# A linear-attention and mixture-of-experts kernel on one core: its computed instruction order replaced by a written-out table

## The chip, the cores and the metric

One Trainium2 chip, one of its cores. The metric is device time in microseconds (us) of one execution; the runs shown give a median and their lowest and highest.

## The reference

Inputs are q, k, v of shape (4, 8, 768, 64) (batch, heads, sequence, head size) and the weights of a four-expert layer. First comes retention, a linear attention with a decaying state; its output, 512 wide, is the x of the second part. There every expert is a causal softmax attention over x with a head of 64; a gate picks two experts for each token and mixes their outputs.

```python
for t in range(S):
    state = gamma[None, :, None, None] * state + np.einsum('bhd,bhe->bhde', k[:, :, t], v[:, :, t])
    y[:, :, t] = scale * np.einsum('bhd,bhde->bhe', q[:, :, t], state)
x = y.transpose(0, 2, 1, 3).reshape(B, S, H * D)
logits = x @ w_gate
# top 2 of 4 experts per token, softmax over the two: w
for e in range(E):
    q, k, v = x @ wq[e], x @ wk[e], x @ wv[e]
    scores = scale * (q @ k.transpose(0, 2, 1))      # causal mask, softmax over keys: a
    out += (weight of e for each token) * (a @ v @ wo[e])
```

## The kernel before, in words

**Retention** runs in 24 chunks of 128 tokens, six to a batch. `chunk` makes three operations on PE (TensorE) of it: `h1`, `h2`, `h1`. `h1` adds 64 tokens to the state in `ps_st` (L486, a matmul of k and v from the tile `kv_t`) and multiplies q with the state so far (L490); the two kinds alternate, 16 calls. In a batch's last `h1` only L490 is left, in its first only L486, 8 calls each. `h2` alternates the products inside a chunk (L545) with the score blocks of the next chunk (L551), 32 calls. All of them are matmuls of 64x64 tiles of float32; one call makes two matmul instructions and two weight loads. So a whole chunk is 64 calls, and where a batch ends and the next begins the two last pieces and the first ones can stand one behind the other. Before a chunk can start, SP must load its `kv_t` (`load`, L414, 512 KB) and `qkT_t` (L410), and POOL (GpSimd) must scale k (`kdecay`, L425) and q (`qdecay`, L440). After each `h1` DVE (VectorE) copies the state out, scaled (L500); after `h2` it masks the score blocks (L559).

**Projections.** Half a batch (384 tokens) is one stage j, eight in all. Its x, split into a rounded part `xh` (ACT, ScalarE, L513) and a rest `xl` (DVE, L516), is multiplied with the weights: `proj` (L601, 12 matmuls for a pair p of experts and e in the pair) gives q and k, `vgate` (L643, 12 matmuls) gives v and the gate's logits. ACT and DVE bring q and k to SBUF (L606, L609), and SP shifts halves of them between partitions by DMA (`move`, L618): two `q<-k`, one `k<-q` that overwrites what the `q<-k` have read and so waits for their landing, one `k<-k`.

**Softmax.** `mpass` (L738, L724, L737) computes scores for the row maximum alone, which DVE takes (L746, L727); `mrow` transposes the maxima on PE (L774), ACT copies them (L776), and SP sends them through DRAM (L778, L780) into row 64 of the q tiles. `score` computes the scores again with that row as an extra term (L850, L851), ACT takes the exponential (L857), `av` multiplies with v (L896). `norm_a` sums over keys on PE (L919, 24 calls of 32 columns), the factors go through DRAM (L933, L937), `norm_b` applies them (POOL, ACT), `wout` (L1010) is the last product, and SP stores 128 rows of the output (L1020).

PE changes its tiling between these: 64x64 for the chunks, 128x64 for L896, 128x32 for L919, 128x128 for the rest. PSUM has six banks for everything passing (`ps`) and one each for the state (`ps_st`) and for L896 (`ps_o`).

**What sets the order.** No operation is emitted at once. `op` records each of them (1,555) with engine, cost, what it reads and writes, and which buffers it begins. `schedule` then plays the program with those costs: at each step, of the operations ready on an engine, the one with the lowest start plus a hundredth of its rank is taken; `shift` has moved the ranks by random numbers of 66 seeds. The result is one list, and it fixes for each engine, SP's queue included, the order in which its instructions stand; each engine works strictly through its own. It also fixes which of a tag's buffers an operation gets. All DMAs are issued by SP, which issues one only when its data and buffer are ready and when the eighth DMA before it has landed; what is queued behind it waits with it.

```python
sc = max(s, T[e]) + ALPHA * o.rank
if e == "PE" and o.mode != mode:
    sc += SWP * SWITCH
...
order = R.schedule()
with tc.manual_schedule():
    for o in order:
        o.fn()
```

## Time and profile before

| | |
|---|---|
| median of 3 runs | 330.72 us (329.74 to 331.65) |
| span of the profiled execution, first to last instruction | 326.7 us |
| median less span (what lies around the instructions) | 4.0 us |
| PE busy with matmuls | 314.3 us, 96% |
| PE weight loads | 272.9 us, 84% |
| DVE, ACT, POOL busy | 53%, 41%, 52% |
| share of PE on the chain that ended last | 88% |
| granted PE clock | full speed, 0.999 in the mean |
| DMA | 50.8 MB, 156 GB/s in the mean |

The profile gives the profiled execution by its span. Busy time of PE counts matmuls that overlap, so a busy engine can still issue more slowly than it might; the distance between two starts tells that. Idle time of an engine that is not the bottleneck costs nothing. "Issue" in the chain is time in which an engine waited for nothing that the profile shows.

### The profile page before, as it was taken

To read this page: it belongs to the slowest core of one execution; us is meant where nothing else is said; L and a number is where in the kernel's file an instruction comes from. 1 tells how busy PE (TensorE), PEld (TensorE's weight loads), DVE (VectorE), ACT (ScalarE), POOL (GpSimd) and SP (SyncE) were. 2 spreads that over 40 slices of the span, in tenths; PEclk is the share of its full clock that TensorE was granted. 3 is DMA by queue.
4 is the path that set the end of the run, shared out by engine and by line. 5 is a ranking of instruction groups with operands and counts; after the bars stand their busy time and mean duration, and the time that the engine had idled before them with its cause. 6 is when DMAs were issued, how large, how long until landed. Compare 5 with 4: busy or idle time off the path is not lost.

```text
span 326.7 us, 11233 instructions
## 1 busy us (share of the span) xinstructions
PE 314.3 (96%) x4738; PEld 272.9 (84%) x4738; DVE 174.7 (53%) x478; ACT 132.6 (41%) x322; POOL 170.3 (52%) x189
## 2 busy tenths in 40 slices
PE   7779999999999999999999999999999999999995
PEld 3669989889978799879979788897979789878674
DVE  2574467666443555767242574937452243896733
ACT  1452222533535333524527224432534235428542
POOL 5776251561874976314785854542394361913700
PEclk9999999999999999999999999999999999999999
DMA  7996993355468353535563675352412422413022
GB/s 261 357 403 226 283 324 117 112 142 179 106 188 266 136 181 102 161 124 181 145 160 135 197 237 144 142 164 86 114 45 99 98 49 74 125 69 91 1 99 96
DMA packets 22071, 50.82 MB, mean 156 GB/s; under 512 B 3618, under 2 KB 8310, under 8 KB 22020
## 3 DMA queue, kind: packets, MB, share of 16 engines
q1 hardware_dynamic: 22020, 50.10, 49.0%
q8 instruction: 37, 0.61, 0.8%
q14 instruction: 14, 0.11, 0.1%
HBM read 30.71 MB, written 6.79 MB: 115 GB/s over the span
## 4 chain that ended last, share of the span: by engine, by line
PE 88%; DMA 7%; issue 1%; SPq 1%; DVE 1%; ACT 1%; ACTq 0%
PE ps L601 20%; PE ps L1010 11%; PE ps_o L896 11%; PE ps L643 9%; PE ps L850 7%; PE ps L851 6%; PE ps_st L486 5%; PE ps L551 4%; PE ps L738 4%; DMA kv_t<-in_kv_dram 3%; PE ps L545 2%; DMA qkT_t<-in_qkT_dram 2%; PE ps L490 2%; PE ps L919 2%; PE ps L724 2%; PE ps_st L896 1%
## 5 line engine op out<-in xcount | busy, mean ns | idle before, releaser
L746 DVE CUSTOM_DVE_ANT_0 scr<-ps,cmask_t 128x128 bf16<-128x128 f32 (+3 forms) x64 | 29.7, 487 | 46.6 <-PE ps L738 46.1
L857 ACT ACTIVATE pt<-ps 128x384 f32<-128x384 f32 (+2 forms) x112 | 49.4, 491 | 12.1 <-PE ps L851 9.7
L440 POOL TENSOR_TENSOR qd<-qkT_t,qdec_t 128x512 f32<-128x512 f32 (+1 forms) x23 | 28.3, 1232 | 41.4 <-PE ps L490 26.2
L601 PE MATMUL ps<-xh,qk_hi 128*128 128x384 f32 x128 | 44.1, 345 | 0.0
L850 PE MATMUL ps<-q,k 128*128 128x384 f32 (+2 forms) x144 | 43.4, 316 | 0.0
L601 PE MATMUL ps<-xh,qk_lo 128*128 128x384 f32 x128 | 43.1, 337 | 0.0
L601 PE MATMUL ps<-xl,qk_hi 128*128 128x384 f32 x128 | 43.1, 336 | 0.0
L851 PE MATMUL ps<-q,k 65*128 65x384 f32 (+2 forms) x144 | 42.1, 312 | 0.0
L879 POOL TENSOR_TENSOR ac<-ac,pt 128x256 f32<-128x256 f32 (+2 forms) x32 | 39.9, 1247 | 3.1 <-ACT pt L857 1.2
L863 POOL TENSOR_SCALAR_AFFINE_SELECT pt<-pt 128x256 f32<-128x256 f32 x48 | 20.1, 426 | 38.9 <-ACT pt L857 38.2
L896 PE MATMUL ps_o<-pt,vt 128*64 128x384 f32 (+2 forms) x252 | 36.2, 422 | 0.0
L606 ACT ACTIVATE k<-ps 128x384 fp32r<-128x384 f32 x32 | 15.7, 491 | 50.0 <-PE ps L601 50.0
L425 POOL TENSOR_TENSOR kv_t<-kv_t,kdec_t 128x512 f32<-128x512 f32 (+1 forms) x23 | 22.2, 968 | 23.0 <-DMA kv_t<-in_kv_dram 23.0
L486 PE MATMUL ps_st<-kv_t 64*64 64x64 f32 x704 | 30.2, 222 | 1.7 <-POOL kv_t L425 0.7
L490 PE MATMUL ps<-qd,sblk 64*64 64x64 f32 x704 | 29.8, 221 | 0.8 <-issue 0.8
L872 POOL TENSOR_TENSOR ac<-pt,pt 128x512 f32<-128x512 f32 (+1 forms) x14 | 21.3, 1523 | 17.5 <-ACT pt L857 17.1
L486 PEld LDWEIGHTS ps_st<-kv_t 64*64 64x64 f32 x704 | 24.9, 134 | 6.2 <-issue 4.0
L896 PEld LDWEIGHTS ps_o<-pt,vt 128*64 128x64 f32 x252 | 16.4, 136 | 16.0 <-issue 11.9
L513 ACT ACTIVATE xh<-ps 128x512 fp32r<-128x512 f32 x24 | 14.3, 598 | 37.4 <-PE ps L490 35.6
L643 PE MATMUL ps<-vg_hi,xh 128*128 128x260 f32 x96 | 28.0, 291 | 1.5 <-ACT xh L513 1.5
L850 PEld LDWEIGHTS ps<-q,k 128*128 128x128 f32 x144 | 27.3, 190 | 2.4 <-issue 2.0
L500 DVE TENSOR_TENSOR sblk<-ps_st,sdec_t 128x256 f32<-128x256 f32 x44 | 18.5, 420 | 19.8 <-PE ps_st L486 18.4
(115 smaller groups left out, 777.6 us busy)
## 6 DMA issues: line engine op xcount, KB each, us to landing
qkT_t<-in_qkT_dram SPq DMA_DIRECT2D x24, 512.0 KB
kv_t<-in_kv_dram SPq DMA_DIRECT2D x24, 512.0 KB
out_dram<-ot SPq DMA_DIRECT2D x24, 256.0 KB
q<-k SPq DMA_DIRECT2D x28, 192.0 KB
k<-k SPq DMA_DIRECT2D x14, 192.0 KB
k<-q SPq DMA_DIRECT2D x14, 192.0 KB
fe<-fd SPq DMA_DIRECT2D x28, 96.0 KB
pt<-in_wqk_dram SPq DMA_DIRECT2D x4, 256.0 KB
```

Of the source, the lines that this page charges most:

```text
L440: e.tensor_tensor(halves(qd.t), halves(qb.t[:, 0]), K["qdec"][:, :, None, :].to_broadcast([128, HP, n, SC]), op=OP.mult)
L486: nc.tensor.matmul(ST[b].t[rows(rt), s * D:(s + 1) * D], kvs(m, 0, s)[rows(rt)], kvs(m, 1, s)[rows(rt)], start=c == 0 and s == 0, stop=Fal ...
L490: nc.tensor.matmul(yo(m, rt, s), SB[m % 2][rows(rt), s], LD[g, 2].t[rows(rt), s, m % 2 * SC:(m % 2 + 1) * SC], start=m % 2 == 0 and s == 0 ...
L601: nc.tensor.matmul(pb.t[:, :HS], ww[:, kt, wsl], xx[:, kt], start=n == 0, stop=n == 11)
L643: nc.tensor.matmul(pb.t[:, :NV + E], xx[:, kt, sl], ww[:, kt], start=n == 0, stop=n == 11)
L746: lambda: nc.vector.tensor_tensor_reduce(scr.t[:, :n1], pb.t[:, :n1], K["cmask"][:, HS + C - n1:], 1.0, mx0.t[:, e, i:i + 1] if prior else ...
L850: nc.tensor.matmul(o, k1.t[:, e, ko:ko + C], q1.t[:, e, q0:], start=True, stop=False)
L851: nc.tensor.matmul(o, k2.t[:65, e, ko:ko + C], q2.t[:65, e, q0:], start=False, stop=True)
L857: lambda es=es, sb=sb, n=n: nc.scalar.activation(pt.t[:, es[0]:es[0] + n, q0:], sb.t[:, :n * w].rearrange("p (e t) -> p e t", e=n), AF.Exp ...
L879: op(eng, cost, lambda: en.tensor_tensor(ac.t[:, :, q0:], ac.t[:, :, q0:], pt.t[:, :, q0:], op=OP.add), r=[(pt, 0), (pt, 1), (ac, "b")], w ...
L896: nc.tensor.matmul(ob.t[e * 64:e * 64 + 64, q0:HS], vt.t[:, ko // C, ee * 64:ee * 64 + 64], pt.t[:, e, q0:], start=kb == 0, stop=kb == las ...
L1010: nc.tensor.matmul(wb.t, oo[:, sl], ww[:, p], start=n == 0 and p == 0, stop=n == 2 and p == NP - 1)
```

## The change

`shift`, `by_path`, `schedule` and `replay` go, with their constants. In their place stands a table of 1,555 numbers, `ORDER`, and for each tag a string of digits, `SLOTS`, that says which buffer each operation's new tile gets; `arrange` lists the operations by them. What is computed, the number of instructions and their shapes stay. For each engine, the operations up to the table's 108th stand as they did; from there on they are moved against each other, on PE by 2.2 places in the mean and 22 at most (510 operations). PE keeps its order for its first 27 operations, up to 39.0 us of the profile before; SP for its first 31, up to 29.9 us.

```diff
@@ -119,155 +95,14 @@
-    def by_path(self, first, scale):
...
-    def shift(self, seeds):
...
-    def schedule(self):
...
+    def arrange(self, order, slots):
+
+        turns = {name: iter(row) for name, row in slots.items()}
+        out = [self.ops[i] for i in order]
+        for o in out:
             for b in o.new:
...
+                b.slot = int(next(turns[b.tag.name]))
         return out
@@ -1160,19 +995,136 @@
-    if PATH:
-        R.by_path(first, PATH)
-    R.shift(SHIFTS)
-    order = R.schedule()
     with tc.manual_schedule():
-        for o in order:
+        for o in R.arrange(ORDER, SLOTS):
             o.fn()
 
+
+ORDER = (
+    2, 1, 3, 4, 5, 6, 7, 8, 9, 10, 11, 12, 13, 14, 15, 16, 17, 18, 81, 22, 19, 20, 0, 21, 23, 99, 100, 101, 102, 103,
...
+SLOTS = {
+    "ac": "010101010101010101",
...
```

The lines of the functions move up by 165 with it: L486 of before is L321 now, L618 is L453.

**First place, PE where the first batch ends and the second begins.** Before (L490 the last piece of the old batch, L486 the first of the new, L551 and L545 the `h2` that follows):

```order
L545 MATMUL ps_142<-am_72,kv_t_68 64x64
L490 MATMUL ps_142<-qd_70,sblk_156 64x64 x8
L486 MATMUL ps_st_147<-kv_t_66 64x64 x8
L551 MATMUL ps_143<-qkT_t_64 64x64
L545 MATMUL ps_140<-am_71,kv_t_66 64x64
```

Now (L325 and L321 are the same two pieces, L573 is `mpass`, L478 is `vgate`):

```order
L380 MATMUL ps_143<-am_72,kv_t_68 64x64
L325 MATMUL ps_143<-qd_70,sblk_156 64x64 x8
L321 MATMUL ps_st_147<-kv_t_66 64x64 x8
L573 MATMUL ps_145<-k_0_83,q_0_77 128x256
L573 MATMUL ps_144<-k_0_83,q_0_77 128x256
L478 MATMUL ps_142<-vg_hi,xh_74 128x260
L478 MATMUL ps_142<-vg_lo,xh_74 128x260
L478 MATMUL ps_142<-vg_hi,xl_76 128x260
```

Before, `h2` and the second `h1` of the new batch's first chunk follow at once, 48 calls; now two `mpass`, a `vgate`, two more `mpass`, a `proj` and a transpose stand ahead of them. At the two other borders of batches `h2` and `h1` followed at once too; now matmuls of L896 (and at the third border an L919 behind them) come between. PE has 76 runs of one tiling before and 82 now.

**Second place, SP's queue around the load of chunk 6, the second batch's first** (`kv_t_66`; L618, now L453, is `move`). Before:

```order
L618 DMA q_0_77<-k_0_83 64x768
L618 DMA k_0_88<-k_0_83 64x768
L618 DMA q_0_77<-k_0_83 64x768
L410 DMA qkT_t_64<-in_qkT_dram 128x1024
L414 DMA kv_t_66<-in_kv_dram 128x1024
L618 DMA k_0_83<-q_0_80 64x768
L618 DMA q_1_78<-k_1_84 64x768 x2
L618 DMA k_1_89<-k_1_84 64x768
```

Now:

```order
L453 DMA q_0_77<-k_0_83 64x768 x2
L245 DMA qkT_t_64<-in_qkT_dram 128x1024
L453 DMA k_0_83<-q_0_80 64x768
L249 DMA kv_t_66<-in_kv_dram 128x1024
L453 DMA k_0_88<-k_0_83 64x768
L453 DMA q_1_78<-k_1_84 64x768 x2
L245 DMA qkT_t_65<-in_qkT_dram 128x1024
L453 DMA k_1_89<-k_1_84 64x768
```

The load of `kv_t_66` stood ahead of the `k<-q` move (`k_0_83<-q_0_80`) and stands behind it now; one `k<-k` move went from ahead of both to behind them. A little further on, the two small transfers of the first mask of maxima (L778, L780), which stood behind two loads and three moves, stand ahead of the next `kv_t` load now, and the first `score` (L850, L851), which reads what they bring, has moved up on PE: between its transpose (L774) and it stand `h2` and `h1` of chunk 6, four `mpass` and a `proj`.

**Third place, SP's queue at the moves of a later stage** (`q_1_78<-k_2_85` and `k_2_85<-q_1_81` are its `q<-k` and `k<-q`; `fe` are the loads of the softmax factors, L937, now L772). Before:

```order
L618 DMA k_2_90<-k_2_85 64x768
L618 DMA q_1_78<-k_2_85 64x768
L937 DMA fe_126<-fd_139 64x384
L618 DMA q_1_78<-k_2_85 64x768
L937 DMA fe_126<-fd_139 64x384 x2
L618 DMA k_2_85<-q_1_81 64x768
L937 DMA fe_126<-fd_139 64x384
L778 DMA md_137<-mt_107 6x128
L780 DMA q_0_80<-md_137 1x768
```

Now:

```order
L453 DMA q_1_78<-k_2_85 64x768 x2
L453 DMA k_2_85<-q_1_81 64x768
L772 DMA fe_126<-fd_139 64x384 x4
L613 DMA md_137<-mt_107 6x128
L453 DMA q_2_79<-k_0_83 64x768
L615 DMA q_0_80<-md_137 1x768
L453 DMA q_2_79<-k_0_83 64x768
L855 DMA out_dram<-ot_128 128x512
```

The two `q<-k` and the `k<-q` stood between the four `fe` loads and stand ahead of all of them now. On PE, the first `mpass` that needs the `k<-q` has the 12 matmuls of another `proj` (L601, now L436) ahead of it that came after it before. The last L919 that followed a chunk's 64 calls at once, at 224.7 us, has four other operations between now; one of an earlier stage, at 73 us, has come to stand behind a chunk.

## Rows read from the trace of the kernel before

**Rows 1.** The page: PE's busy line, and the queue that brings instructions.

```profile
PE 314.3 (96%) x4738; PEld 272.9 (84%) x4738; DVE 174.7 (53%) x478; ACT 132.6 (41%) x322; POOL 170.3 (52%) x189
...
q8 instruction: 37, 0.61, 0.8%
```

**Rows 2.** Busy time by stretch: length, then each engine's, clock, DMA share, GB/s.

```profile
40.00:280.00 240.00, 237.63 (x3676) 212.08 (x3676) 126.04 (x354) 97.25 (x239) 130.67 (x139) 1.00 0.48 146
```

**Rows 3.** The same view, of four stretches of 64x64 matmuls.

```profile
43.09:45.94 2.85, 2.10 (x103) 1.75 (x99) 1.93 (x4) 0.51 (x1) 2.17 (x2) 1.00 0.91 255
94.27:96.29 2.02, 2.02 (x129) 1.95 (x128) 1.44 (x6) 0.47 (x1) 0.74 (x2) 1.00 0.71 256
110.61:112.36 1.75, 1.75 (x102) 1.62 (x98) 1.52 (x4) 0.51 (x1) 1.67 (x2) 1.00 0.69 176
186.41:188.95 2.54, 2.07 (x103) 1.81 (x99) 1.86 (x4) 0.51 (x1) 1.88 (x2) 1.00 0.82 235
```

**Rows 4.** Timeline of PE at borders: start us, us, engine line op.

```profile
39.04 0.34 PE L643 MATMUL ps<-vg_hi,xh 128*128 128x260 f32 x1
...
40.54 0.40 PE L738 MATMUL ps<-k,q 128*128 128x256 f32 x2
40.87 0.27 PE L486 MATMUL ps_st<-kv_t 64*64 64x64 f32 x1
...
50.90 0.41 PE L738 MATMUL ps<-k,q 128*128 128x256 f32 x2
51.15 0.29 PE L643 MATMUL ps<-vg_hi,xh 128*128 128x260 f32 x1
...
94.78 0.22 PE L551 MATMUL ps<-qkT_t 64*64 64x64 f32 x1
...
261.06 0.27 PE L774 MATMUL ps<-ident_t,mx 128*128 128x128 f32 x1
```

**Rows 5.** The chain that ended last: start us, us, what.

```profile
44.75 0.75 issue
...
147.11 0.79 PE ps L919 x24
...
188.10 0.47 issue
...
192.21 2.10 PE ps L601 x12
...
224.70 0.78 PE ps L919 x21
225.48 0.38 issue
225.86 0.41 PE ps L919 x3
```

**Rows 6.** PE's waits: engine line waited for, us in total, times, longest.

```profile
PE ps L738 <- DMA k<-q: 0.8, 1, 0.8
```

**Rows 7.** Timeline of SP: DMA issues at two places.

```profile
30.58 0.59 SPq L618 DMA_DIRECT2D q<-k  x1
...
31.91 0.52 SPq L414 DMA_DIRECT2D kv_t<-in_kv_dram  x1
35.17 0.47 SPq L618 DMA_DIRECT2D k<-q  x1
...
261.66 0.29 SPq L778 DMA_DIRECT2D md<-mt  x1
262.86 0.25 SPq L780 DMA_DIRECT2D q<-md  x1
```

**Rows 8.** Timeline of POOL around 38 us; in brackets idle before, releaser.

```profile
37.59 0.74 POOL L440 TENSOR_TENSOR qd<-qkT_t,qdec_t 128x256 f32<-128x256 f32 x1 [4.70 <-DMA kv_t<-in_kv_dram]
38.28 1.04 POOL L425 TENSOR_TENSOR kv_t<-kv_t,kdec_t 128x512 f32<-128x512 f32 x1
```

**Rows 9.** SP's own waits, as in rows 6.

```profile
SPq L780 <- DMA md<-mt: 12.1, 9, 2.1
```

## The prediction

> **What bounds the kernel now.** I read the page of the profile first. PE is busy for 96% of the span [rows 1], so only three things can move the time: idle time of PE, time in which it issues more slowly than it could, and what the first 39 us and the last few hold, which the change hardly touches (PE's order is the same up to 39.0 us). Then the busy time by stretch: between 40 and 280 us PE is idle for 240 - 237.63 = 2.4 us [rows 2]. That is all that better-placed waits can win there, so I looked inside the busy time as well, at starts on the timeline and at the chain of waits.

> The 64x64 matmuls show what is to be found. An ordinary chunk, 64 calls, takes 2.02 us [rows 3]. Its `h2` begins at 94.78 [rows 4], so `h2` and the last `h1`, 48 calls, take 96.29 - 94.78 = 1.51 us. Where one batch ends and the next begins, the same 48 calls follow 64 others at once, and there they take 2.85, 1.75 and 2.54 us [rows 3]. In two of the three PE stands still for 0.75 and 0.47 us with "issue" as the reason [rows 5], waiting for nothing that the profile shows; the rest of the excess is slower issue. A third stop of this kind, 0.38 us, cuts an L919 in two; that one also follows a chunk's 64 calls at once [rows 5].

> What could be late there is the program itself. The queue that brings instructions moved 0.61 MB in 37 transfers [rows 1]; over PE's 4738 matmuls and as many weight loads that is 64 bytes each, so an estimated 256 instructions to a transfer. An ordinary chunk uses up 257 (129 and 128) in 2.02 us [rows 3]; the whole program takes one transfer in 326.7 / 37 = 8.8 us. So a chunk eats instructions four times as fast as the mean, and only a second dense piece right behind it has shown a stop.

> **The change, part by part.**

> *Dense runs are taken apart.* At all three borders `h2` and `h1` now stand behind other work. Before, they took 2.85 + 1.75 + 2.54 = 7.14 us; standing alone I take the ordinary 1.51 each, 4.53. That wins 2.6 us. It costs six more changes of PE's tiling (76 runs become 82). Two L738 of 256 columns take 51.15 - 50.90 = 0.25 us when the same tiling follows and 40.87 - 40.54 = 0.33 when a 64x64 run does [rows 4], 0.08 more, which I round up to 0.1 a change and 0.6 in all. Net -2.0. The other end: if the stops stay wherever the matmuls stand, only the slower issue goes, and the net is near 0.

> [...]

> *L919 away from a chunk.* The 24 calls of an L919 take 0.79 us when nothing stops them, and 0.78 + 0.38 + 0.41 = 1.57 at 224.7 [rows 5]. With four operations between, I take the 0.78 as won. The other end is 0: an L919 at 73 us has come to stand behind a chunk, and it may stop there. I take the gain since the one at 147.11, also right behind a chunk, was not stopped [rows 5].

> *The wait for a `k<-q`.* One L738 waits 0.8 us for that DMA [rows 6]. Now the moves go ahead of the factor loads in SP's queue, and a `proj` of 2.10 us [rows 5] stands ahead of the L738. That covers the 0.8 whole: -0.8, with 0 as the other end if the moves are later than before. The factor loads that are passed have slack: they feed POOL, and PE reads of them much later.

> *A load behind a move.* The load of `kv_t` for chunk 6 was issued at 31.91 and ended POOL's wait just before 37.59, 5.7 us later [rows 7, 8]. Now it stands behind the `k<-q`, which was issued at 35.17 [rows 7] since it waits for the `q<-k` of 30.58 to land; that one moves up by one issue, 0.6 us. So the load goes at 35.1 to 35.7 and lands, after the same 5.7 us, at 40.8 to 41.4; L425 on POOL adds 1.04 [rows 8]. PE meanwhile has brought the old batch's last chunk forward: it started at 40.87, behind the `vgate` of 39.04 [rows 4], and starts at 39.1 now; the new batch's first L486 came an estimated 1.8 us after that start (2.22 to the `h2` at 43.09 [rows 3], less 0.4 for itself), so PE stands before it at 40.9. It waits for 0.9 to 1.5 us if the flight is as long as it was. Between that and 0, if the load flies faster with less ahead of it, I take 0.8. Behind this L486 all of PE waits.

> *The first row of maxima.* The first `score` has moved up. From L774 to L778 takes 0.6 us, and the next transfer L780 goes 1.2 us later [rows 4, 7]; with as much again for its landing the way takes 3.0. SP's waits for such a transfer reach 2.1 us, 2.4 with its issue [rows 9], which makes 0.6 + 2.4 + 2.4 = 5.4. Between the transpose and the first use PE now has 1.51 for `h2` and `h1`, 2.10 for a `proj`, 0.2 for two changes of tiling and an estimated 0.6 for four `mpass` and the first L850: 4.4 us. So the wait is 0 to 1.0. DMA is 0.91 busy around there [rows 3], which speaks for the slow end: +0.4.

> *Swaps on DVE and ACT.* Neighbours changed places all over both queues; their work is the same. In a queue that waits in order, a swap makes PE wait for at most the instruction that was let ahead, about 0.48 us on DVE (1.93 for four) or 0.51 on ACT [rows 3]. I found three places where PE reads right behind such a swap: a `proj` behind `xl` near 44 us, a `vgate` that needs a PSUM bank back near 61, an L896 near 305. A third of 0.5 each makes +0.5, with 0 and 1.5 as ends.

> *Removed code* runs on no engine: the planner worked while the kernel was built. Cost 0.

> **The sum:** -2.0 - 0.8 - 0.8 + 0.8 + 0.4 + 0.5 = -1.9 us. The profiled span of 326.7 becomes 324.8. The runs' median, 330.72, is 4.0 above the span, and I leave those 4.0 as they are: **328.8 us**, 0.6% less. About 0.5%, 1.65 us, is what a measurement of this kernel can tell from no change.

> **Rivals.**

> *The stops move instead of going.* If the "issue" stops come from where transfers of instructions begin and end and not from how dense the calls stand, other places will be hit. For it: the middle border had no stop with the same 112 calls [rows 3], and the third border's `h2` now stands right behind an L919, 72 calls in a row. Against it: in 40 to 280 us every stop was behind more than 64 dense calls. Then 0.75 + 0.47 + 0.78 = 2.0 us of the gain are gone: 330.8, no change. [...] Rows 5 show the stops, no row their cause.

> *Lateness is handed on in SP's queue (slower).* All loads go through one queue, and a `k<-q` that waits holds everything behind it. If the `kv_t` load is not only late once, but the next two, which use the two other buffers of that tile, are late behind it, PE pays at three chunks. It decides at 39.9 us: a load that lands later than that (40.9 less POOL's 1.04) is paid in full. At 41.4 the first costs 1.5; three such are 4.5 instead of my 0.8: -1.9 + 3.7 = +1.8, 332.5. For it: DMA is 0.91 busy at 43 to 46 us [rows 3]. Against it: from 40 to 280 us the share is 0.48 in the mean [rows 2], and a load that waits for its buffer is early by then.

> *The new waits don't come.* Each of the three costs has 0 as its lower end. Without them the gain is 3.6: 327.1.

> That the order isn't what the table says is excluded: the listed instructions show it.

> **How the numbers follow.** The forecast's case gets 0.54, the moved stops 0.21, lateness 0.13, no new waits 0.12. Around its 328.8 the first case spreads by about a microsecond, so a third of it (0.20) is within 0.5% and two thirds (0.34) faster. Faster by over 0.5%: 0.34 + 0.12 = 0.46; within: 0.20 + 0.21 = 0.41; slower: 0.13. The range goes from just under the case without new waits, 326.9, to the lateness case, 332.6, which leaves out about half of each.

> **What would show it.** Right: the two pieces at the borders take near 1.5 us each with no "issue" in them, PE is never idle for 0.8 before that L738, and a wait of PE for POOL's L425 near 41 us is the longest after 40 us. Wrong: "issue" pieces of half a microsecond at other places, PE idle above 2.4 us in 40 to 280, or L486 waiting at several chunks.

## The result, and the profile after

The runs of after took 327.40 us in the median (327.19 to 327.87, four runs), those of before beside them 331.19 (329.74 to 332.65, four runs): ratio 0.9898, 95% interval 0.9861 to 0.9935, a gain of 3.8 us where 1.9 were forecast (328.8). Medians, here and below, are of all runs of a kernel, while ratios leave out those over 1.5% above its fastest, among them the executions that the traces of e1 and e8 show. The profiled execution of after has a span of 325.7 and took 327.45, so 1.75 us lie around the instructions, in its other runs too. By that the profiled execution of before took 326.7 + 1.75 = 328.5, less than any of before's four runs: the 4.0 us that I took to lie around the span were 1.75, and the rest was a quick execution.

The page of after, its busy time between 40 and 280 us, and PE's waits in that stretch, in this order (the last row: engine line waited for, us in total, times, longest):

```profile
span 325.7 us, 11215 instructions
...
PE 315.0 (97%) x4738; PEld 272.6 (84%) x4738; DVE 172.2 (53%) x478; ACT 129.8 (40%) x322; POOL 170.1 (52%) x189
...
q8 instruction: 37, 0.61, 0.8%
```

```profile
40.00:280.00 240.00, 239.09 (x3683) 212.33 (x3682) 124.77 (x360) 95.13 (x241) 130.85 (x139) 1.00 0.48 144
```

```profile
PE ps L380 <- issue: 0.7, 1, 0.7
```

PE is idle for 240 - 239.09 = 0.9 us there, against 2.4 [rows 2], and it waits for a cause that the profile names no longer: the wait for `k<-q` [rows 6] is gone, and neither a load nor the row of maxima has taken its place. The spans differ by 1.0 us only, though, so the time around the two executions has to be looked at too. Stretches are compared best between places of PE's order ahead of which both orders have done the same operations. There are such places near 39, 65, 157, 198 and 238 us; the last matmul is the sixth. (The operation that stands at the place may differ.) PE's starts there, on the timeline, in after, in a run with the order of before (e5 below), and the first two in before itself:

```profile
39.61 0.22 PE L573 MATMUL ps<-k,q 128*128 128x128 f32 x1
...
66.82 0.44 PE L436 MATMUL ps<-xh,qk_hi 128*128 128x384 f32 x1
...
159.01 0.28 PE L685 MATMUL ps<-q,k 128*128 128x256 f32 x1
...
199.50 0.27 PE L685 MATMUL ps<-q,k 128*128 128x256 f32 x1
...
238.40 0.22 PE L321 MATMUL ps_st<-kv_t 64*64 64x64 f32 x1
...
321.80 0.39 PE L845 MATMUL ps<-wo_hi,ol 128*128 128x512 f32 x1
```

```profile
39.97 0.22 PE L573 MATMUL ps<-k,q 128*128 128x128 f32 x1
...
67.01 0.34 PE L436 MATMUL ps<-xh,qk_hi 128*128 128x384 f32 x1
...
159.26 0.28 PE L685 MATMUL ps<-q,k 128*128 128x256 f32 x1
...
200.72 0.27 PE L609 MATMUL ps<-ident_t,mx 128*128 128x128 f32 x1
...
241.68 0.22 PE L321 MATMUL ps_st<-kv_t 64*64 64x64 f32 x1
...
326.55 0.40 PE L845 MATMUL ps<-wo_hi,ol 128*128 128x512 f32 x1
```

```profile
38.87 0.22 PE L738 MATMUL ps<-k,q 128*128 128x128 f32 x1
...
64.97 0.34 PE L601 MATMUL ps<-xh,qk_hi 128*128 128x384 f32 x1
```

The distances of such starts, from all traces whose instructions stand at their own places (before, after, e5 to e11), by the order that the stretch had, and the sum of my terms for it:

| stretch | order of before | order of after | difference of means | forecast |
|---|---|---|---|---|
| start to 39 (same order) | 38.87 to 42.72, nine traces, median 39.68 | | | 0 |
| 39 to 65 | 25.71 to 28.95, mean 26.81 (7) | 27.21, 26.11 | -0.2, within the scatter | +0.4 |
| 65 to 157 | 92.00 to 92.35, mean 92.14 (7) | 92.19, 92.28 | +0.1 | 0.0 |
| 157 to 198 | 41.22 to 41.52, mean 41.36 (6) | 40.48, 40.49, 40.49 | -0.88 | -0.83 |
| 198 to 238 | 39.56 to 40.96, mean 40.14 (6) | 38.90, 38.90, 38.84 | -1.26 | -1.6 |
| 238 to the last start | 84.33, 84.32 (before, e7) | 83.40, 83.40 | -0.93 | +0.2 |

The gain stands behind 157 us, and adds up to 3.1 us there. (With the buffers of e5, e6 and e9 the last stretch took 84.87; e10 and e11 have waits of their own in it, told below.) From 157 on the order of after repeats its times to a few hundredths; the order of before scatters. Ahead of that everything is even. Before's head of 38.87 was the earliest of the nine, 0.8 below their median, and its stretch to 65 us was 1.1 shorter than after's (26.10 against 27.21): that is why its span came out only 1.0 above after's.

The border of batches as I had drawn it, `h2` and the second `h1`, busy time by stretch of after (length, then as in rows 2), against 2.85, 1.75 and 2.54 [rows 3]:

```profile
47.93:49.49 1.56, 1.56 (x98) 1.49 (x97) 0.28 (x1) 0.27 (x1) 0.33 (x1) 1.00 0.65 251
114.15:115.71 1.56, 1.56 (x99) 1.49 (x97) 0.35 (x1) 0.00 (x0) 1.48 (x3) 1.00 0.51 165
189.59:191.15 1.56, 1.56 (x100) 1.49 (x96) 1.03 (x2) 0.37 (x1) 0.30 (x1) 1.00 0.99 394
```

They take 4.68 us instead of 7.14, as forecast (4.53). But at the first border a stop stands elsewhere now. The chain of after:

```profile
41.49 0.71 issue
42.20 0.27 PE ps L380
...
60.61 1.28 DVE gs L515
61.94 0.11 issue
62.04 0.37 ACT pt L692
62.41 0.30 ACT ac L710
62.71 0.28 ACT vt L494
63.00 0.04 issue
63.04 0.44 PE ps L685
```

The stop of 0.71 us is one call from the end of an `h2`, only 47 calls into dense work (from start to start it is 0.93). And near 62 us PE follows ACT, which follows the gate's long DVE work: its starts are late by 0.28 and 0.23 us there. That is close to one of the three swaps I had feared, though a `score` is late (L685) and not the `vgate` that I had named.

### The profile page after: what moved, and what is told of

The parts are those of the page before. It is cut to its first block, busy times and chain, and to the rows that moved or that the text cites. A ratio compares the mean times of both kernels' runs of the same rounds, so it can differ in the third digit from the quotient of the medians.

```text
span 325.7 us, 11215 instructions
## 1 busy us (share of the span) xinstructions
PE 315.0 (97%) x4738; PEld 272.6 (84%) x4738; DVE 172.2 (53%) x478; ACT 129.8 (40%) x322; POOL 170.1 (52%) x189
## 4 chain that ended last, share of the span: by engine, by line
PE 91%; DMA 2%; DVE 2%; issue 2%; SPq 1%; ACT 1%; ACTq 0%
PE ps L436 20%; PE ps L845 11%; PE ps_o L731 11%; PE ps L478 10%; PE ps L685 7%; PE ps L686 7%; PE ps_st L321 5%; PE ps L386 5%; PE ps L573 4%; PE ps L380 2%; PE ps L325 2%; PE ps L559 2%; PE ps L754 2%; PE ps_st L731 1%; DMA ot<-in_wvg_dram 1%
## 5 line engine op out<-in xcount | busy, mean ns | idle before, releaser
L436 PE MATMUL ps<-xh,qk_hi 128*128 128x384 f32 x128 | 43.9, 343 | 0.0
L685 PE MATMUL ps<-q,k 128*128 128x384 f32 (+2 forms) x144 | 43.8, 319 | 0.1
L436 PE MATMUL ps<-xl,qk_hi 128*128 128x384 f32 x128 | 43.2, 338 | 0.0
L436 PE MATMUL ps<-xh,qk_lo 128*128 128x384 f32 x128 | 43.2, 337 | 0.0
L686 PE MATMUL ps<-q,k 65*128 65x384 f32 (+2 forms) x144 | 42.3, 313 | 0.0
L731 PE MATMUL ps_o<-pt,vt 128*64 128x384 f32 (+2 forms) x252 | 35.8, 422 | 0.0
L380 PE MATMUL ps<-am,kv_t 64*64 64x64 f32 x768 | 27.6, 219 | 2.9 <-issue 2.9
L321 PE MATMUL ps_st<-kv_t 64*64 64x64 f32 x704 | 29.5, 221 | 0.7 <-issue 0.7
L731 PEld LDWEIGHTS ps_o<-pt,vt 128*64 128x64 f32 x252 | 16.5, 136 | 15.8 <-issue 12.1
L478 PE MATMUL ps<-vg_hi,xh 128*128 128x260 f32 x96 | 28.1, 292 | 1.5 <-ACT xh L348 1.5
L685 PEld LDWEIGHTS ps<-q,k 128*128 128x128 f32 x144 | 27.3, 190 | 2.5 <-issue 1.2
L325 PE MATMUL ps<-qd,sblk 64*64 64x64 f32 x704 | 29.4, 221 | 0.0
```

Source lines behind the costliest of these rows:

```text
L321: nc.tensor.matmul(ST[b].t[rows(rt), s * D:(s + 1) * D], kvs(m, 0, s)[rows(rt)], kvs(m, 1, s)[rows(rt)], start=c == 0 and s == 0, stop=Fal ...
L325: nc.tensor.matmul(yo(m, rt, s), SB[m % 2][rows(rt), s], LD[g, 2].t[rows(rt), s, m % 2 * SC:(m % 2 + 1) * SC], start=m % 2 == 0 and s == 0 ...
L380: nc.tensor.matmul(yo(2 * g + u, rt, s), kvs(u + 2 * g, 1, s)[rows(rt)], amg.t[rows(rt), u, s], start=g % NC == 0 and u == 0 and s == 0, s ...
L436: nc.tensor.matmul(pb.t[:, :HS], ww[:, kt, wsl], xx[:, kt], start=n == 0, stop=n == 11)
L478: nc.tensor.matmul(pb.t[:, :NV + E], xx[:, kt, sl], ww[:, kt], start=n == 0, stop=n == 11)
L685: nc.tensor.matmul(o, k1.t[:, e, ko:ko + C], q1.t[:, e, q0:], start=True, stop=False)
```

## The experiments

**Why "issue"?** Counting all of PE's instructions in order of start (9476 matmuls and weight loads, and between them 60 others in before and 65 in after, nearly all on semaphores), the three stops of before stand behind instruction 1985, 6593 and 7617, that of after behind 1729. All are 193 more than a multiple of 256, the estimated size of one transfer of q8 (in before 9476 matmuls and weight loads over 37 transfers). The first four runs move every later instruction against these borders by a longer warm-up at the head, and change no order: by 92 instructions in e1 (on before) and e4 (on after), by 196 in e2 (on before), by 36 in e3 (on after). The first edit is that of e1 and e4, the second that of e2; e3's is the second with 22 short matmuls instead of 102:

```diff
-            for i in range(12):
-                nc.tensor.matmul(pbs[i % 6].t, wu, wu[:, None, :].to_broadcast([128, 4, 128]), start=True, stop=True)
+            for i in range(58):
+                nc.tensor.matmul(pbs[i % 6].t[:, :106], wu, wu[:, :106], start=True, stop=True)
```

```diff
-            for i in range(12):
+            for i in range(8):
...
+            for i in range(102):
+                t = slice(i % 2 * 64, i % 2 * 64 + 64)
+                nc.tensor.matmul(pbs[i % 6].t[t, :16], wu[t, :64], wu[t, :16], start=True, stop=True)
```

> The order of before, with 58 warm-up matmuls of 106 columns instead of 12 of 512 (same columns, 92 more instructions on PE), so that every later instruction stands 92 places further on. Theory A (the supply of instructions: PE stops at a border of 256 instructions when the 256 before it ran in under about 2.8 us): the stops of 44.5, 187.8 and 225.2 us (0.97, 0.68, 0.66) go from there, and by the times of before's trace the 256 instructions that begin at 41.4, 98.6, 109.5, 145.2, 164.7, 184.8 and 237.2 us ran in 2.44, 2.82, 2.41, 2.10, 2.62, 2.41 and 2.92 us, which makes stops near 43.9, 111.9, 147.3, 167.3 and 187.2 us of 0.5 to 1.0 each and small ones near 101 and 240: about 4.0 us of stops after 39 us instead of 2.3, so the time is 1.5 to 2 us above before. Theory B (the stop belongs to the dense run, wherever the borders are): stops stay at 44.5, 187.8 and 225.2 with their sizes, and the time is before's within 0.5.

Measured: 342.42 us, ratio 1.0293 (1.0238 to 1.0347). PE's four longest waits behind 39 us in e1, then the two largest stops and the 256 instructions ahead of each:

```profile
PE ps L551 <- issue: 3.8, 1, 3.8
PE ps L919 <- issue: 2.5, 1, 2.5
PE ps_st L486 <- issue: 2.4, 3, 1.1
PE ps L545 <- issue: 0.8, 1, 0.8
```

```profile
48.35:50.83 2.48, 2.48 (x143) 2.35 (x136) 1.90 (x6) 0.60 (x1) 0.73 (x1) 1.00 1.02 317
50.83:54.83 4.00, 0.22 (x15) 0.08 (x8) 0.50 (x1) 0.00 (x0) 1.59 (x2) 1.00 0.87 266
159.12:161.32 2.20, 2.20 (x139) 2.13 (x136) 1.12 (x3) 0.62 (x2) 0.15 (x1) 1.00 0.93 371
161.32:164.05 2.73, 0.27 (x7) 0.01 (x1) 1.02 (x2) 0.41 (x1) 2.12 (x2) 1.00 0.90 297
```

The six stops here stand at 50.8, 112.9, 124.8, 161.3, 205.5 and 260.4, each behind instruction 256 n + 193; counted in instructions, five are the listed ones (the later clock time comes from what was lost ahead of them), two of the list are missing, one is new. None is left where before had its own. So theory B falls. But the sizes of A were far too small: 10.8 us in six stops, not 4 (in the trace, which is of the longest of the seven runs), and the time is some 10 us above before instead of 1.5 to 2. One more "issue" wait, of 0.8 us ahead of an L738 at 45.8 (in e2 1.4, at 44.3), is at no such border, and its cause stays open.

> The order of before, with 110 warm-up matmuls (8 of 512 columns, 102 of 16) instead of 12: every later instruction stands 196 places further on. Theory A: the three stops of before go; what is left after 39 us are a stop near 111 us of about 0.7 (its 256 instructions took 2.38 us in before) and one near 71.5 of up to 0.3 (2.81 us): 1.0 us instead of 2.3, the time 1 to 1.5 us below before. Theory B: stops stay at 44.5, 187.8 and 225.2; time as before within 0.5.

Measured: 339.24, ratio 1.024 (1.0187 to 1.0292). The stops moved again, and the one forecast near 111 came (0.69, at 117.4). But stops of 0.86, 0.87 and 1.20 came behind 256 instructions that had taken 4.15, 3.91 and 5.68 us, and one of 3.07 behind 2.58, at 196.5. A fixed limit of 2.8 us is wrong, and the time, forecast 1 to 1.5 us below before, came out 8 above it.

> The order of after, with 30 warm-up matmuls (8 of 512 columns, 22 of 16) instead of 12: later instructions stand 36 places further on. Theory A: no 256 instructions of after between two borders run in under 3.2 us then, so its one stop after 39 us (0.93 at 41.3) goes or falls under 0.3, and the time is 0.5 to 0.9 below after's 327.4: about 326.6. Theory B (the stop at 41.3 belongs to that piece of the order): it stays, time 327.4 within 0.3.

Measured: 332.82, ratio 1.0072 (1.004 to 1.0104). A miss: the stop stayed at the border behind instruction 1729 (1.42 us, 256 instructions in 3.66), and one of 1.05 came at 113.3. The edit also disturbed the head: granted clock 0.85 in the mean of the first 14 us and 0.95 from there to 39, since it stood at 0.50 for part of them, and PE at the place near 39 us 2.2 us later than in after.

> The order of after, with 58 warm-up matmuls of 106 columns instead of 12 of 512: later instructions stand 92 places further on. Theory A: the 256 instructions that begin at 100.9, 147.1, 166.7, 219.9 and 237.1 us ran in 2.82, 2.25, 2.62, 2.02 and 2.93 us in after, which makes stops near 103.7, 149.4, 169.3, 221.9 and 240 of 0.3, 0.85, 0.5, 1.1 and 0.2: about 3 us instead of 0.9, the time near 329.4. Ordinary chunks with nothing dense behind them would then stop too. Theory B (only runs of more than 64 dense calls stop): no new stops, 327.4 within 0.5.

Measured: 340.24, ratio 1.0278 (1.0231 to 1.0325). Ordinary chunks stop too: 3.46 us at 156.9 and 1.03 at 109.9, the listed places. The stops forecast near 169 and 222 did not come, after's own near 41 stayed and grew (1.84, at 46.3), and the time was forecast at 329.4. In e1 and e4 the place near 39 us came some 6 us later, at 45.8 and 45.3, in part by stops of 3.1 and 3.4 us at such a border near 17 us.

What sets the size is seen with the transfers of q8 beside the stops. In all 58 stops of over 0.6 us at such a border in the 14 traces, PE resumed 1.24 to 1.64 us after the end of a q8 transfer; at none of 505 borders, stop or not, did it pass sooner than 1.21 us after the end of the transfer for what follows. Where the data queues were nearly idle (DMA share under 0.3 from the border before up to the transfer's start, 13 stops), the transfer began 0.1 to 1.2 us after that border; with a share of 0.81 and more (43 stops) 0.6 to 5.2 us after it. In the stop of 4.0 us in e1 it began 3.44 us after the border. The shortest of these delays, 0.1, with 0.9 for a transfer and 1.2 behind it, make an estimated 2.2 us for 256 instructions, and more where the delay was longer (up to 5.2). It is no fixed limit: where the transfer began 1.2 us ahead of the border before, in e4 near 234.9, two borders stood 2.12 us apart with a stop of 0.1. At 447 of the 505 borders there was no such stop; ahead of the 58, PE had run 256 instructions in 2.2 to 5.7 us.

The stops alone don't make e1 and e4 so slow. Behind e1's two longest after 39 us, and behind e4's longest, the clock that PE was granted fell to 0.50 for 3.41 us (busy time by stretch of e1, twice, and of e4; PEclk stands ahead of the last two numbers):

```profile
54.96:58.37 3.41, 3.41 (x69) 3.29 (x67) 1.67 (x6) 0.60 (x1) 1.46 (x2) 0.50 0.46 148
164.19:167.60 3.41, 3.41 (x21) 3.00 (x17) 1.74 (x3) 0.98 (x2) 0.61 (x1) 0.50 0.17 65
```

```profile
161.63:165.04 3.41, 3.41 (x12) 3.41 (x12) 2.79 (x6) 0.74 (x2) 1.99 (x3) 0.50 0.55 175
```

Two of these stretches cost an estimated 1.7 and 1.8 us: from the place near 65 to that near 157, e1 took 98.82 us, 6.7 more than the mean of before's order, while its three stops there make 4.9; e4 took 98.50, 6.3 more than after's order, while its two stops make 4.5. Behind e2's stop of 3.07 and behind those of up to 2.3 us after 39 us the clock stayed at 1.00. In the heads of e1, e2, e3 and e4 it stood at 0.50 for 6.8, 3.4, 6.8 and 10.2 us, so by my estimate a good part of what the shifts cost is clock. The same shows in the times of before: of its 76 runs beside the experiments, the 50 with a mean granted clock of 0.998 or more have a median of 330.47, the other 26 one of 333.26. After's four runs were at 0.998 and more; against 330.47 their 327.40 is 3.1 less, which is what the stretches add up to. What lowered the clock in the 26 is not shown, since none of them was traced.

**Where the gain is.** The next runs have the code of after with other tables. e5 has before's order for all engines; e6, e7 and e8 have after's order in one stretch and before's elsewhere (where their expectations round my terms otherwise than the table above, the table is right). Buffers are given out anew, least recently used first. e5 against after:

```diff
 ORDER = (
...
-    134, 133, 136, 161, 164, 163, 180, 166, 150, 142, 162, 165, 208, 135, 138, 152, 137, 139, 151, 124, 126, 209,
+    151, 150, 124, 126, 226, 209, 210, 125, 127, 143, 145, 227, 228, 144, 153, 146, 165, 155, 154, 157, 156,
```

> The code of after with the order of before written out as its table (every engine's sequence is that of before). Both theories: the time of before within 0.5%, so the removed planner costs nothing. Theory A (supply of instructions) also says that the stops stand at the same instructions as in before (first seen at 44.5, 187.8 and 225.2 us), with a size that follows the transfer of the next 256 instructions: the stop ends 1.2 to 1.6 us after its last packet. If that transfer starts late behind other traffic, the stop is larger than the 0.66 to 0.97 of the profile of before, up to 3 us, and that is where the runs' median above that profile and their scatter come from. Theory C (the runs lose it elsewhere, in the head or in waits for loads): stops of 0.7 to 1.0 again and the rest at other places.

Measured: 332.37, ratio 1.0048 (1.0009 to 1.0087): before's time, or half a per cent above it (one wait of 0.3 us of L731 for POOL is new with the other buffers). PE's waits behind 39 us:

```profile
PE ps L325 <- issue: 1.8, 1, 1.8
PE ps L573 <- DMA k<-q: 1.4, 1, 1.4
PE ps_st L321 <- issue: 0.5, 1, 0.5
PE ps L754 <- issue: 0.5, 1, 0.5
```

The stops are at the same instructions, and the first takes 1.8 us where before's had 0.75 [rows 5]; the wait for `k<-q` is 1.4 where it was 0.8 [rows 6]. Theory A holds here, and C in part: the head is 1.1 us later as well.

> The order of after up to 66 us (the first border between batches), that of before behind it. By the traces: the stop of 0.97 at 44.5 and some 0.4 of slower issue go, a stop of 0.9 at 41.3 and 0.5 of waits near 62 come, so within 0.5 us of the table with before's order if the stops keep their size; if the stop at 44.5 is what makes before scatter, up to 2 us faster and with less scatter. My prediction for this part was -0.9 (border) +0.8 +0.4 +0.3 = +0.6 us.

Measured: 331.88, ratio 1.0034 (0.9997 to 1.0071). That is 0.5 below e5, so nothing clear is won at the first border.

> The order of after from 66 to 157 us (the second border), that of before elsewhere. By the traces there was no stop to win there: 0 to -0.3 us against the table with before's order, same scatter. My prediction for this part: -0.1.

Measured: 330.85, ratio 1.0 (0.9959 to 1.004), before's time. It is 1.5 below e5, more than the 0 to 0.3 expected, but not by this stretch: it took 92.28 us, no less than with before's order (92.14 in the mean).

> The order of after from 157 us on (third border, the wait for the move from q to k, the L919 at 225), that of before up to there. By the traces the stops of 0.68 and 0.66, the wait of 0.88 and 0.65 of small ones near 288 go: -2.2 to -2.9 us against the table with before's order. My prediction for this part was -1.0 -0.8 -0.8 = -2.6, less 0.2. If the late stops are what makes before scatter, more than that and with the scatter of after.

Measured: 327.37, ratio 0.99 (0.9852 to 0.9947). The order from 157 us on gives the whole gain, 3.7 us against before's median beside it and 5.0 against e5's, where 2.2 to 2.9 were expected. It is the order and not the buffers: from there on 196 of the 263 operations on PE, DVE and ACT that begin a tile have another buffer than in after, and the three stretches take what they take in after, to 0.01 us.

**Which part behind 157 us.** The table of e5, with after's order in one shorter stretch each:

> The order of after from 157 to 198 us only (the third border), that of before elsewhere. My prediction for this part: -0.8 us. The traces with before's order there lose 0.95, 0.97, 1.12 and 1.35 us to stops and slow issue between 157 and 199 us, those with after's order nothing: -1.0 to -1.4 us in the trace, about 330 in the runs; the stop of 0.7 near 188 us is gone, the wait of 0.7 to 1.5 near 203 and the small ones near 288 stay.

> The order of after from 198 to 238 us only (the moves ahead of the factor loads, a proj ahead of the L738, the L919 away from the chunk), that of before elsewhere. My prediction for this part: -0.8 -0.8 = -1.6 us. The traces with before's order there lose 1.72, 2.50, 1.05 and 1.03 us between 199 and 236 us, those with after's 0.2 to 0.3: -0.8 to -2.2 us, about 329.5 in the runs. If the k<-q only waits elsewhere now, a wait of PE for it of over 0.3 us shows in the trace.

> The order of after from 238 us to the end only, that of before elsewhere. My prediction for this part: nothing won, +0.2 us for a swap ahead of an L896. Against it, the traces with before's order lose 1.24 to 1.7 us behind 236 us (0.21 and 0.44 around the first wout near 288, 0.20 near 315, the rest small), those with after's 0.23: -1.0 us in the trace. The three parts together should make up the 3.7 us that the order from 157 us on won.

Measured: e9 333.61, ratio 1.0077 (1.0039 to 1.0115); e10 332.19, 1.0014 (0.9972 to 1.0055); e11 342.75, 1.0315 (1.0252 to 1.0379). The runs cannot resolve the parts: against e5 (332.37) e9 is 1.2 above and e10 even. The traces can, since they show the stretch itself: 40.49 us between 157 and 198 in e9 (41.46 in e5), and 38.84 between 198 and 238 in e10 (40.96), with no wait for `k<-q`. But e9's L919 stop was 1.22 us, and e10 has a wait of its own behind the seam, 1.0 us for DVE's `sblk` at 243. In e11 the seam spoils the run. Its waits of PE from 238 to 253 us:

```profile
PE ps_o L731 <- POOL pt L698: 7.5, 3, 6.2
```

A `k<-q` stands between `fe` loads in SP's queue at this seam, POOL waits 3.3 us for the `fe` load and has its exponentials' masks behind it. This tells nothing of the change, so what the last part wins rests on e8 and after (83.40 both), not on a run of it alone. It does show lateness in SP's queue reaching PE by way of POOL, at a cost of 6.2 us in one wait, which was my slower rival's way; from 247.68 on the clock was at 0.50 there too, for 10.24 us.

**A version of its own.** e12 puts one `vgate` back ahead of the chunk whose `h2` is stopped in after:

```diff
-    210, 125, 153, 155, 181, 230, 154, 157, 127, 184, 143, 144, 145, 226, 158, 228, 156, 227, 183, 146, 147, 159,
+    150, 124, 126, 209, 226, 153, 210, 125, 151, 155, 154, 127, 157, 184, 165, 158, 183, 143, 145, 181, 144,
```

The `vgate` is 226, and the chunk's three pieces are 153, 155 and 157. The list is written in another sequence across engines; on PE only 226 has moved, and each other engine's order is that of after.

> The order of after with one vgate (24 instructions, 1.44 us) moved from behind the last chunk of the first batch to ahead of it, where before had it. The border of instructions near 41 us then closes 256 instructions that take about 5.0 us instead of 3.66. If the transfer that brings the next ones starts about 2 us into them, as in after, the stop of 0.93 near 41 us goes: 326.5 to 327.0 against after's 327.4. If it starts 3 us or more into them, as in two other runs, a stop of up to 1 us is left: 327.4. If a new wait for the moved vgate's input or bank appears on PE, slower than after.

Measured: 327.82, ratio 0.9917 (0.9885 to 0.9949), no better than after. The stop at 41 us is gone; waits that add up to 0.9 us are there instead. PE's waits from 43.5 to 47 us:

```profile
PE ps L436 <- DVE xl L351: 0.4, 1, 0.4
PE ps L436 <- DVE am L394: 0.3, 1, 0.3
PE ps L573 <- DVE mx L581: 0.2, 1, 0.2
```

No version beat after.

## Why the prediction was right in direction and half the size

*Dense runs taken apart, -2.0.* The matmuls that were moved gave the 2.5 us forecast (7.14 to 4.68). At the third border that is a gain: -0.88 in its stretch, -0.83 forecast, e9 alone the same. What a change of tiling costs isn't separated: the two pieces gained 0.98 there (2.54 to 1.56), the stretch 0.1 less, where I had put 0.2 for two changes. At the first border nothing came of it: the 1.3 us won there were given back as a stop of 0.93 at 41.3, in after, and as small waits. That this stretch came out near its forecast all the same (-0.2, forecast +0.4) is luck, since the costs that I had set against the gain stayed away too. The cause I gave, a second dense piece behind a first, was wrong. The 58 stops stood at borders of 256 instructions, 2.2 to 5.7 us after the border before, and in 56 of them the transfer had begun 0.1 to 5.2 us after that border; density was only one way to that. An "issue" piece at another place was one of my own signs of being wrong, and it came. What I had put down as the rival that the stops move "if they come from where transfers of instructions begin and end" was the right mechanism (e1 to e4), with the wrong time: two of before's three stops had no successor.

*L919 away from a chunk, -0.8.* That stop was 0.66 and 0.72 us in before and e5, 1.22 in e9, 0.4 in e11 and under 0.25 in e6 and e7, where its transfer ended 1.1 to 1.2 us after the border before, not 1.5 as in before; with after's order it never came. Right, and somewhat too large.

*The wait for `k<-q`, -0.8.* Right: 0.6 to 1.4 us in six traces with before's order (mean 0.8), none at that place in those with after's. (In e1 and e2, whose instructions are shifted, there was none either.) The two terms came to -1.26 in their stretch, instead of -1.6.

*The load behind the move, +0.8.* It did not come; the step that failed is the time of the issue. SP and POOL of after, on the timeline:

```profile
34.12 0.46 SPq L453 DMA_DIRECT2D k<-q  x1
34.68 0.54 SPq L249 DMA_DIRECT2D kv_t<-in_kv_dram  x1
```

```profile
40.19 1.04 POOL L260 TENSOR_TENSOR kv_t<-kv_t,kdec_t 128x512 f32<-128x512 f32 x1 [1.14 <-DMA kv_t<-in_kv_dram]
```

The `k<-q` was issued at 34.1, and the load at 34.68, not at 35.1 to 35.7 (I had moved it up by one issue only, from 35.17 [rows 7]); POOL had its data 5.5 us later, the 5.7 forecast, and was done at 41.23. PE, whose head was 0.7 later and which had the stop of 0.9, came to that L321 at 42.61. Without either it would have come at 40.9 and waited for some 0.3 us, so that in after no wait came of it is in part luck. In e6, whose head was not late, POOL was done at 39.47 and PE there at 41.20.

*The first row of maxima, +0.4.* It did not come. The transfers were issued at 48.33 and 50.81 and the row was there at 52.28, 4.55 us after the transpose, not 5.4; I had the second transfer's way 0.9 too long. PE came to the L686 that reads it at 52.5, as forecast (4.4 us for the first `score`).

*Swaps, +0.5.* One of the three came, near 62 (or one like it), with the 0.5 us that I had for all. The sign was wrong in the last part: I had bounded swaps by 0 and 1.5, so left out that one could win, and it won 0.93. In before the first L1010 comes at the end of a chain over DVE (the chain of before, start us, us, what):

```profile
286.43 0.30 DVE f L925
286.73 0.47 DVE scr L746
287.20 0.95 DVE mx L727 x2
288.15 0.04 issue
288.20 0.97 PE ps L1010 x3
```

PE's starts are late by 0.21 and 0.44 us there, 0.65 of the 0.93; where the rest lay is open. In after the transpose of the gate (L704, now L539) runs 5 us earlier, and no start is late at that place. The bound should have been drawn from -1 to +1.5.

*The rival without new waits (327.1)* gave the time nearest to 327.4, and the waits did stay away. But it also took the first border for won; that 1.1 us was made up by the last part, which it didn't have. The base was an error of another kind: the sum was made against one execution whose head and first border were quick, and then put on the median.

## What to carry to other kernels

Look at stops that the profile calls "issue" by counting the engine's instructions, and put the transfers of the program beside them. Here the stops stood behind instruction 256 n + 193 and ended 1.24 to 1.64 us after such a transfer, so I took them for the supply of the program; 36 to 196 instructions more at the head left the borders where they were in the count and put other work there. These edits cost 1.7% to 3.9%, more than the new order was worth, and a part of that was the lower clock in the head and behind long stops; so look at the granted clock beside the stops. Compare kernels that differ in order by stretches between places where the same work is done, in several executions; the sum of one profile was off by 2.3 us here for its base alone. When a reordering is priced, swaps need a bound on the side of a gain too.
